# Threshold attention and a feed-forward block on one core: where summed weights are kept, when they and v are loaded, and the order of four products

## The chip, the cores and the metric

The kernel runs on one core of a Trainium2 chip. The time is the device time of one execution in microseconds (us), as the median of several runs: 1335.26 us over three runs (1334.43 to 1337.13). A profile is one more execution, recorded by the hardware profiler.

## What is computed

For each of 8 batches and 8 heads (576 tokens, 64 features a head) the attention keeps only the scores within `tau` of a row's maximum. The result is the input of a normalised two-layer block with 512 features in, 2048 hidden, 512 out. All data are float32.

```
scores = q @ k.T / 8
scores = where(scores >= max(scores) - tau, scores, -1e9)
attn = exp(scores - max); attn = attn / (sum(attn) + 1e-9)
x = attn @ v                         # heads side by side: (8, 576, 512)
xn = (x - mean) / sqrt(var + 1e-6) * g_ln
out = x + relu(xn @ w_ch1) @ w_ch2
```

## The kernel before, in words

**Slots and groups.** Attention is cut into nine slots for each batch, numbered 0 to 8 here (72 in all): slots 0 to 3 and 5 to 8 are a pair of heads with half of the queries, slot 4 is the rest of the queries of all heads. The feed-forward block is cut into 16 groups of 288 tokens, two for each batch. Its steps are a generator, and the main loop deals them out to the four quarters of each slot (`second_part`, L1322, by `dealt` and `STEPS`), so that TensorE (PE) always has something to multiply between the pieces of attention. An even group takes slots 7 and 8 of its batch and 0 and 1 of the next; an odd group takes slots 2 to 6. In what follows group two is the even group of the second batch.

**One slot of attention.** PE makes the scores (L434); VectorE (DVE) takes the negated row maxima (L450); GpSimd (POOL) makes the threshold (L454); ScalarE (ACT) writes four exponentials into the tile `e` (L463); DVE masks them against the scores in four instructions (L473, "masks"); POOL divides them (L490); DVE transposes 32x32 blocks in place (L559). One DMA then stores `e` to a scratch tensor in DRAM (`scr<-e`, L580, 1152 KB), and in the next slot a DMA brings it back in another layout (`em<-scr`, L594, 1024 KB, and `er<-scr`, L599). PE multiplies that by v (L638, L649). There is one tile `e` for all slots, so the exponentials of a slot wait until the store of the slot before has landed.

**The SP queue.** Nearly all DMAs are issued by SyncE (SP), in the order in which the program names them. A wait of one holds all behind it. In a slot the order is: `em<-scr` and two `er<-scr`; four stores of results (`out_dram<-ot`); in slots 8, 0, 1 and 2 four loads of q and four of k for the next pair of heads (L120), which wait until DVE has transposed the old ones (L368 to L378); loads of summed weights (L891); the store `scr<-e`; in slots 7, 8, 0 and 1 the load of v for the next batch: `v_in` (L135, 256 KB) and two `v_rest` (L144, 32 KB each).

**Sums in place of products.** From group two on, a part of the first layer is made by a scheme of Winograd's kind. A "unit" (`unit`, L940) takes four of the 16 hidden tiles and makes them with seven products of half size instead of eight: 28 half steps instead of 16 whole ones. A whole step multiplies a 128x128 weight by 288 columns, a half step by 144. Each appears in the program as two matmuls of 64 columns of weights and in the trace as four MATMUL records. A group has three units (hidden tiles 0 to 3, 4 to 7 and 12 to 15) and four plain tiles (8 to 11). The second layer is made in the same manner from group one on, in seven segments (`second_quarters`, L1136).

A unit needs twelve 128x128 sums of weights (768 KB). They are made once, by DVE and POOL, from the weights (`sums_of_w1`, L893), one twelfth at every ninth step of group one's second layer, and stored in DRAM. Two rooms in SBUF take them in turn: room 0 is `extra[:, :12]`, room 1 is the rest of `extra`, the end of an unused `e` tile and `ident`, so that a load into room 1 is three DMAs. A room is refilled from DRAM for every unit of every group (`load_sums`, in quarter 1 of the slot after the unit, which is ahead of the masks).

The seven products of a unit are named p1 to p7. p6, p7 and the last one are added up in one PSUM bank (`chain`), and between them ACT copies it out (L979, L983). p3 and p5 have banks of their own. The order is p6, p5, p7, p3 in the first unit of a group and p5, p6, p3, p7 in the others (L994).

**Rooms that bound the order.** PSUM has two banks for the feed-forward block (`ps_ff`); a bank is free again when ACT has copied it out. After every group the means are subtracted by DVE (`centre`, L742), and the next group's first products wait for that.

Of the kernel before, what the change touches and what calls it, by code (L numbers as in the profile page):

```python
# [18 lines left out]
def kernel(  # L19
# [106 lines left out]
            tiles.append(t)  # L126
        loaded[u] = tuple(tiles)

    def load_v(u):
        b, hp = units[u]  # L130
        vt = ins.tile([128, 2, J, D], F32, tag="v", name="v_in")
        vr = v_rest[hp]
        both = v[b, 2 * hp : 2 * hp + 2]
        if b:
            nc.sync.dma_start(  # L135
                out=vt.rearrange("p h c d -> p h (c d)"),
                in_=both[:, : J * 128].rearrange("h (p c) d -> p h (c d)", c=J),
            )
        for h in range(0 if b else 2):
            nc.sync.dma_start(  # L140
                out=vt[:, h], in_=both[h, : J * 128].rearrange("(c p) d -> p c d", p=128)
            )
        for j in range(2):
            nc.sync.dma_start(  # L144
                out=vr[64 * j : 64 * j + 64, j], in_=both[:, J * 128 :].rearrange("h p d -> p h d")
            )
        values_in[u] = (vt, vr)
# [319 lines left out]
    def weights(n, es, thr, divide):  # L467


        den = small.tile([128, 4], F32, tag="den", name="den")  # L470
        for i in range(4):
            e = blocks_of(es, i, n)
            nc.vector.scalar_tensor_tensor(  # L473
                out=e, in0=like(blocks[i], n), scalar=thr[:, i : i + 1], in1=e,
                op0=ALU.is_ge, op1=ALU.mult, accum_out=den[:, i : i + 1],
            )
            if divide and i % 2:
                nc.vector.reciprocal(den[:, i - 1 : i + 1], den[:, i - 1 : i + 1])  # L478
        if not divide:
            nc.vector.reciprocal(den, den)  # L480
        diags = []
        for i in range(4):
            if not divide:
                if i % 2 == 0:
                    two = ffn.tile([128, TOK], F32, tag="o", bufs=4, name="diag")
                diags.append(two[:, i % 2 * 128 : i % 2 * 128 + 128])
                nc.scalar.mul(diags[i], ident, den[:, i : i + 1])
                continue
            e = blocks_of(es, i, n)
            nc.gpsimd.tensor_scalar(  # L490
                out=e, in0=e, scalar1=den[:, i : i + 1], scalar2=1.0,
                op0=ALU.mult, op1=ALU.mult,
            )
        return diags
# [350 lines left out]
                    yield  # L845

    UNITS = (((0, 1), (2, 3)), ((4, 5), (6, 7)), ((12, 13), (14, 15)))
    PLAIN = [d for d in range(ND) if all(d not in t for u in UNITS for t in u)]
    sums_due = []
    last_added = set()  # L850

    def unit_slots(g):
        n, i = divmod(ready(g), QUARTERS)
        return [n + (i > 0) + k for k in range(len(UNITS))]

    PIECES = 12
    stored = [
# [20 lines left out]
        at, pieces = [r for r in rooms_of(room) if r[0] <= i][-1]  # L878
        return pieces[:, i - at]

    def room_for(g, k):

        return (len(UNITS) * g + k) % 2

    def store_sums(k):
        for at, pieces in rooms_of(room_for(2, k)):
            nc.sync.dma_start(out=stored[k][:, at : at + pieces.shape[1]], in_=pieces)

    def load_sums(g, k):
        for at, pieces in rooms_of(room_for(g, k)):  # L890
            nc.sync.dma_start(out=pieces, in_=stored[k][:, at : at + pieces.shape[1]])  # L891

    def sums_of_w1():  # L893


        for k, (f1, f2) in enumerate(UNITS):
            for c in range(2):
                for m in range(2):
                    cols = [slice(128 * t[m], 128 * t[m] + 128) for t in (f1, f2)]
                    a11, a12 = (w1_sb[2 * j + c][:, cols[0]] for j in range(2))  # L900
                    a21, a22 = (w1_sb[2 * j + c][:, cols[1]] for j in range(2))
                    if k < 2:
                        p2, p3, p4 = (piece_of(room_for(2, k), i, c, m) for i in range(3))
                    else:
                        two = [ffn.tile([128, TOK], F32, tag="o", bufs=4, name="sum") for _ in range(2)]
                        p2, p3, p4 = two[0][:, :128], two[0][:, 128:256], two[1][:, :128]
                    for eng, out, a, b, op in (
                        (nc.vector, p3, a11, a21, ALU.subtract),
                        (nc.vector, a21, a21, a22, ALU.add),
                        (nc.vector, p2, a21, a11, ALU.subtract),  # L910
                        (nc.gpsimd, p4, a12, p2, ALU.subtract),
                    ):
                        eng.tensor_tensor(out=out, in0=a, in1=b, op=op)
# [3 lines left out]
            if k < 2:  # L917
                store_sums(k)

    sums_of_x = {}  # L920

# [18 lines left out]
    def unit(g, xc, k):  # L940


        f1, f2 = UNITS[k]
        t1, t2, t3, t4 = sums_of_x[g]
        of = lambda f, j: hidden[:, f[0] : f[0] + 2, (early, late)[j]]
        h11, h12, h21, h22 = of(f1, 0), of(f1, 1), of(f2, 0), of(f2, 1)
        w_of = lambda f, j: lambda c, m: w1_sb[2 * j + c][:, 128 * f[m] : 128 * f[m] + 128]
        s_of = lambda which: lambda c, m: piece_of(room_for(g, k), which, c, m)
        x_of = lambda i, j: lambda c: xc[:, 2 * i + c, (early, late)[j]]
        t_of = lambda t: lambda c: t[:, c]  # L950
        other = [
# [39 lines left out]
            steps(other[1], s_of(2), x_of(1, 1), True, True),  # L991
            lambda: sums_due.append(lambda: add(h12, other[1], h12)),
        )
        order = (p5, p6, p3, p7) if k else (p6, p5, p7, p3)  # L994
        for i, (part_of, after) in enumerate(order):
            for end in part_of:
                if end:
# [30 lines left out]

    def unit_and_load(g, k):
        yield from second_half(g, k)  # L1030
        n = max(now // QUARTERS, unit_slots(g)[k])
        yield from unit(g, centred[g], k)
        h, i = divmod(len(UNITS) * g + k + 2, len(UNITS))
        if h < NG:
            at_quarter(max(n, now // QUARTERS) + 1, 1, load_sums, h, i)

    def first_units(g):


        xc = centred[g]  # L1040
        sq = hidden[:, ND - NK :]
        due = False
        for k in range(2):
            for d in PLAIN[2 * k : 2 * k + 2]:
# [17 lines left out]
            yield from unit_and_load(g, k)  # L1062
            if k == 0:
                due = now >= QUARTERS * NS
                if not due:
# [70 lines left out]
    def second_quarters(g, rb):  # L1136
# [87 lines left out]
        t2 = "t2", 3, by_fours, dve if g == 1 else pool, b11, b11, b12, ALU.add  # L1224
        if g == 1:
            later(t3, urgent=pool)
            banks_taken[0] = True
        yield from segment(w2[0, 0], b11, y11)
        if g == 1:
            need("t3")  # L1230
            later(t2, urgent=dve)
        yield 2, 0.5
        if g > 1:
            yield from unit_and_load(g, 2)
            sums_of_x.pop(g)
# [46 lines left out]

    def ffn_steps(g):
        rb = yield from (first_part if g < 2 else first_units)(g)
        sums = sums_of_w1() if g == 1 else iter(())
        for i, step in enumerate((second_quarters if g else second_plain)(g, rb)):
            if i % 9 == 8:
                next(sums, None)
            yield step

# [3 lines left out]


    ROOM = (0.6, 1.0, 1.25, 0.35)
    STEPS = [0.5 + NK * ND * 2] + [0.5 + NK * ND * 2 - NK * ND // 8] + [
        0.5 + NK * ND * 2 - NK * ND // 8 - 2 * len(UNITS)
    ] * (NG - 2)
    ends = [sum(STEPS[: i + 1]) for i in range(NG)]  # L1300
    queue = []
    issued = part = now = 0
# [19 lines left out]
    def second_part(n, i):  # L1322
# [13 lines left out]
        else:  # L1336
            if i == 0:
                share = remain / (ready(g + 1) // QUARTERS - n)
                if has_unit and n < unit_slots(g)[2]:
                    dealt[:] = [4, 4, UNIT_COST - 2, 2]  # L1340
# [12 lines left out]
        least = 2 if has_unit and i < 2 and n < unit_slots(g)[2] else 0.5  # L1353
# [82 lines left out]
    for n in range(NS):  # L1436
# [49 lines left out]
        if n < SLOTS:  # L1486
            run_all(stores)
        conversion.begin_to(behind_at)
        run(n, 2)
        second_part(n, 2)  # L1490
        if n < FIRST:
# [93 lines left out]
```

## Time and profile before

| what | from | value |
|---|---|---|
| median of three runs | the times | 1335.26 us (1334.43 to 1337.13) |
| the profiled execution | the times | 1337.87 us |
| its span, first to last instruction | the page | 1336.1 us |
| granted TensorE clock, mean | the page | 0.990 |
| PE busy / DVE / ACT / POOL | the page | 1280.0 / 961.8 / 528.6 / 674.2 us |
| DMA engines, mean rate | the page | 186 GB/s, 248.06 MB |
| loads of sums | the page's DMA issues | 20 of 768 KB; 20 of 576 KB, 20 of 128 KB and 20 of 64 KB |
| store `scr<-e` | the page's DMA issues | 60 of 1152 KB, median 5.2 us to landing |

A busy PE is the union of its matmul records, so its idle time is what the first table of the page leaves: 1336.1 - 1280.0 = 56 us. "Waits" lists, for an engine and a line, who ended its idle time. A timeline row gives start, duration, engine, line and operation, and in brackets the idle time before it. A row of SPq is the issue of a DMA, not its transfer. A landing is told by the DMA views.

### The profile page before, as it was taken

Reading aid. Unit: us, or ns where it says so; the run is one execution under the profiler, and the core shown is the slowest. Engines: PE = TensorE matmul, PEld = TensorE weight load, DVE = VectorE, ACT = ScalarE, POOL = GpSimd, SP = SyncE. Lnnn points to the kernel's source line nnn. Section 1 sums busy time; section 2 is a strip of 40 time slices with the busy share of each in tenths; the row PEclk is TensorE's granted clock in tenths of the full one; section 3 lists DMA queues with packets and bytes.
Section 4 is the critical chain, followed back from the end, with each engine's and each line's share of the span. In section 5 each row is a group of like instructions: output and inputs, shape, how many; then the busy total and the mean of one; then the engine's idle time right before and its main releaser. Section 6 shows DMA issues by size and latency. Waiting matters only on the chain.

```text
span 1336.1 us, 45057 instructions
## 1 busy us (share of the span) xinstructions
PE 1280.0 (96%) x19320; PEld 1090.4 (82%) x19320; DVE 961.8 (72%) x1762; ACT 528.6 (40%) x1191; POOL 674.2 (50%) x890
## 2 busy tenths in 40 slices
PE   8899889889999999999999999999999999999997
PEld 6765457778898898988989888987979888898987
DVE  7979888985777858785877857777576857777123
ACT  5866342243433424342343424334243423434131
POOL 3465565544545454554535455453445545455423
PEclk9999899999999999999999999999999999999999
DMA  8937865567765776657666667648676576565311
GB/s 151 292 116 186 205 165 175 199 175 208 219 207 184 220 208 207 222 166 211 182 213 206 196 165 228 212 169 215 197 216 208 175 201 182 187 224 185 85 43 20
DMA packets 349144, 248.06 MB, mean 186 GB/s; under 512 B 248912, under 2 KB 301136, under 8 KB 340880
## 3 DMA queue, kind: packets, MB, share of 16 engines
q1 hardware_dynamic: 342832, 244.29, 61.9%
q8 instruction: 152, 2.49, 0.8%
q10 hardware_dynamic: 5952, 0.74, 0.4%
q0 software_dynamic: 160, 0.15, 0.1%
q14 instruction: 48, 0.39, 0.1%
HBM read 155.45 MB, written 89.65 MB: 183 GB/s over the span
## 4 chain that ended last, share of the span: by engine, by line
PE 66%; DMA 4%; DVE 3%; ACT 2%; POOL 2%; issue 2%; POOLq 0%; ACTq 0%; DVEq 0%; SPq 0%
PE seg L103 27%; PE chain L103 10%; PE p L103 8%; PE sc L434 7%; PE sc L638 7%; PE sc L103 5%; DMA scr<-e 4%; DVE e L473 2%; ACT e L463 1%; PE sc L649 1%; DVE neg L450 1%; POOL e L490 1%; DMA v_in<-in_v_dram 1%; POOL q_in L350 0%; POOL sum L692 0%
## 5 line engine op out<-in xcount | busy, mean ns | idle before, releaser
L450 DVE TENSOR_REDUCE neg<-sc 128x2 f32<-128x1152 f32 x144 | 190.0, 1353 | 153.9 <-PE sc L434 150.9
L490 POOL TENSOR_SCALAR e<-e,den 128x576 f32<-128x576 f32 x264 | 206.1, 792 | 116.8 <-DVE den L478 116.7
L103 PE MATMUL p<-xc,w 128*64 128x288 f32 (+1 forms) x2080 | 233.4, 374 | 18.8 <-ACT y L1181 13.9
L103 PE MATMUL seg<-hidden,w 128*64 128x144 f32 x3840 | 246.6, 287 | 0.0
L103 PEld LDWEIGHTS seg<-hidden,w 128*64 128x64 f32 x3840 | 234.6, 137 | 10.4 <-issue 10.2
L473 DVE SCALAR_TENSOR_TENSOR e<-sc,thr,e 128x576 f32<-128x576 f32 x288 | 222.4, 810 | 26.3 <-ACT e L463 13.2
L103 PEld LDWEIGHTS p<-xc,w 128*64 128x64 f32 x2080 | 139.4, 138 | 100.2 <-ACT y L1181 15.5
L463 ACT ACTIVATE e<-sc,neg 128x576 f32<-128x576 f32 x288 | 196.4, 754 | 22.2 <-DMA scr<-e 17.9
L559 DVE STREAM_TRANSPOSE e<-e 128x1152 f32<-128x1152 f32 (+1 forms) x113 | 163.8, 1451 | 22.8 <-POOL e L490 22.4
L1166 POOL TENSOR_TENSOR hidden<-hidden 128x576 f32<-128x576 f32 x88 | 122.6, 1419 | 97.4 <-ACT hidden L1008 88.6
L454 POOL TENSOR_SCALAR thr<-neg,low_sb 128x2 f32<-128x2 f32 x144 | 39.7, 276 | 252.8 <-DVE neg L450 250.8
L434 PE MATMUL sc<-kT,qT 64*64 64x384 f32 (+3 forms) x2048 | 139.6, 403 | 2.9 <-DVE e L473 1.6
L638 PE MATMUL sc<-em,v_in 128*64 128x128 f32 (+1 forms) x2368 | 131.9, 265 | 5.1 <-DVE e L473 3.0
L638 PEld LDWEIGHTS sc<-em,v_in 128*64 128x64 f32 x2368 | 122.9, 138 | 9.1 <-DVE e L473 4.5
L103 PE MATMUL seg<-hidden,stage 128*64 128x144 f32 x1920 | 123.1, 286 | 0.4 <-ACT part L1181 0.4
L103 PEld LDWEIGHTS seg<-hidden,stage 128*64 128x64 f32 x1920 | 117.2, 137 | 3.2 <-issue 2.5
L434 PEld LDWEIGHTS sc<-kT,qT 64*64 64x64 f32 x2048 | 76.6, 133 | 43.4 <-issue 21.2
L103 PE MATMUL chain<-t,extra 128*64 128x144 f32 x1344 | 99.2, 291 | 0.0
L1181 ACT COPY part<-seg 128x288 f32<-128x288 f32 x74 | 30.0, 407 | 156.1 <-PE seg L103 133.4
L103 PEld LDWEIGHTS chain<-t,extra 128*64 128x64 f32 x1344 | 86.8, 140 | 0.0
L663 ACT COPY x<-sc 128x128 f32<-128x128 f32 x120 | 31.1, 267 | 127.8 <-PE sc L434 71.3
L1022 POOL TENSOR_TENSOR hidden<-hidden 128x288 f32<-128x288 f32 x48 | 38.8, 808 | 75.4 <-ACT hidden L1386 73.9
(165 smaller groups left out, 1774.0 us busy)
## 6 DMA issues: line engine op xcount, KB each, us to landing
scr<-e SPq DMA_DIRECT2D x60, 1152.0 KB, 5.2
em<-scr SPq DMA_DIRECT2D x63, 1024.0 KB, 5.8
extra<-sums SPq DMA_DIRECT2D x20, 768.0 KB, 6.4
extra<-sums SPq DMA_DIRECT2D x20, 576.0 KB, 5.1
out_dram<-ot SPq DMA_DIRECT2D x248, 36.0 KB, 3.9
q_in<-in_q_dram SPq DMA_DIRECT2D x120, 72.0 KB, 2.5
er<-scr SPq DMA_DIRECT2D x132, 64.0 KB, 5.2
k_in<-in_k_dram SPq DMA_DIRECT2D x116, 72.0 KB, 2.9
```

Source lines behind the costliest of these rows:

```text
L103: nc.tensor.matmul(out[r], lhsT=lhsT[:, r], rhs=rhs, **flags)
L434: mm = nc.tensor.matmul(sc[h][64 * i : 64 * i + 64, at : at + n], lhsT=ql[r] if s == HP else qT[r, half, j * 128 + 64 * i : j * 128 + 64 * ...
L450: nc.vector.tensor_reduce(out=neg[:, i], in_=pairs[h], axis=AXL.X, op=ALU.max, negate=True,)
L454: nc.gpsimd.tensor_scalar(out=thr[:, i], in0=neg[:, i], scalar1=-1.0, scalar2=low_sb, op0=ALU.mult, op1=ALU.add,)
L463: nc.scalar.activation(blocks_of(es, i, n), like(blocks[i], n), func=AF.Exp, bias=neg[:, i : i + 1])
L473: nc.vector.scalar_tensor_tensor(out=e, in0=like(blocks[i], n), scalar=thr[:, i : i + 1], in1=e, op0=ALU.is_ge, op1=ALU.mult, accum_out=de ...
L490: nc.gpsimd.tensor_scalar(out=e, in0=e, scalar1=den[:, i : i + 1], scalar2=1.0, op0=ALU.mult, op1=ALU.mult,)
L559: nc.vector.transpose(et[:, :, at], et[:, :, at])
L638: mm = nc.tensor.matmul(dst[64 * h : 64 * h + 64], lhsT=vt[:, h, c, :], rhs=pick(em[:, 2 * j : 2 * j + 2, c], h), start=c == 0 and first, ...
L663: nc.scalar.copy(x_of(2 * b + (s > HP))[:, s % (HP + 1), 128 * j : 128 * j + 128], pv[j])
L1022: nc.gpsimd.tensor_tensor(out=sq[:, 0], in0=sq[:, 0], in1=sq[:, c], op=ALU.add)
L1166: eng.tensor_tensor(out=out[at], in0=in0[at], in1=in1[at], op=op)
```

## The change

1. **v.** In slots 7, 8, 0 and 1 the load of v for the next batch is issued ahead of the store `scr<-e` instead of behind it, and its first DMA (`v_in`) waits for the second of the slot's four masks.
2. **Rooms.** Room 1 holds the sums of the second unit for good. Room 0 is refilled for the first and third unit in turn, each time with one DMA of 768 KB, in quarter 2 of the slot after the unit, behind the second mask. That makes 25 loads instead of 40 (of one or three DMAs). In slots 8 and 1 the load stands behind v and ahead of `scr<-e`.
3. **Group two** has two units, and hidden tiles 12 to 15 are plain: three plain tiles ahead of each unit and two behind. No sums are loaded for it. The sums of the first two units are made in group one, at every 13th step; those of the third in group two's second layer, at every 24th step, and stored from there. Group two's second layer starts as group one's does.
4. **Order.** After the last slot all units have the order p6, p5, p7, p3.

```diff
+    masked = []
+
+    def behind_masks(request):
+        if masked:
+            tc.add_manual_dep(
+                request.ins, masked[-1].ins.name,
+                mybir.DependencyInfo(mybir.DependencyClass.Sync, mybir.DependencyReason.ANTI),
...
     def weights(n, es, thr, divide):
...
+            if i == 1:
+                masked[:] = [mask]
...
+    def load_sums(k):
+        behind_masks(nc.sync.dma_start(out=extra[:, :PIECES], in_=stored[k]))
+        in_room[0] = k
+
+    def units_of(g):
+
+        return 2 if g == 2 else 3
...
-        s_of = lambda which: lambda c, m: piece_of(room_for(g, k), which, c, m)
+        s_of = lambda which: lambda c, m: piece_of(k % 2, which, c, m)
...
-        order = (p5, p6, p3, p7) if k else (p6, p5, p7, p3)
+        order = (p5, p6, p3, p7) if k and now < QUARTERS * NS else (p6, p5, p7, p3)
...
     def unit_and_load(g, k):
         yield from second_half(g, k)
-        n = max(now // QUARTERS, unit_slots(g)[k])
         yield from unit(g, centred[g], k)
-        h, i = divmod(len(UNITS) * g + k + 2, len(UNITS))
-        if h < NG:
-            at_quarter(max(n, now // QUARTERS) + 1, 1, load_sums, h, i)
+        if k == 1 or g == 2 or (g, k) == (NG - 1, 2):
+            return
+        if now < QUARTERS * NS:
+            at_quarter(now // QUARTERS + 1, 2, load_sums, 2 - k)
+        else:
+            load_sums(2 - k)
...
+        tiles = ((8, 9, 10), (11, 12, 13), (14, 15)) if g == 2 else ((8, 9), (10, 11), ())
...
-        sums = sums_of_w1() if g == 1 else iter(())
+        sums = sums_of_w1({1: (0, 1), 2: (2,)}.get(g, ()))
         for i, step in enumerate((second_quarters if g else second_plain)(g, rb)):
-            if i % 9 == 8:
+            if i % (13 if g == 1 else 24) == (12 if g == 1 else 23):
                 next(sums, None)
...
         conversion.begin_to(behind_at)
+        if n >= SLOTS - 2 and (n + 2) % SLOTS < HP and n < NS - 2:
+            load_v((n + 2) // SLOTS * HP + (n + 2) % SLOTS, behind_masks)
         run(n, 2)
         second_part(n, 2)
...
-        elif n >= SLOTS - 2 and (n + 2) % SLOTS < HP and n < NS - 2:
-            load_v((n + 2) // SLOTS * HP + (n + 2) % SLOTS)
```

More of the change, by code (lines that the diff above doesn't have):

```diff
@@ L127, in load_qk, with load_v @@
         loaded[u] = tuple(tiles)
-    def load_v(u):
+    masked = []
[4 more added lines that the diff above has]
+                mybir.DependencyInfo(mybir.DependencyClass.Sync, mybir.DependencyReason.ANTI),
+                reason="not beside the turned weights",
+            )
+    def load_v(u, behind=lambda request: None):
         b, hp = units[u]
@@ L134, in load_v @@
         if b:
-            nc.sync.dma_start(
-                out=vt.rearrange("p h c d -> p h (c d)"),
-                in_=both[:, : J * 128].rearrange("h (p c) d -> p h (c d)", c=J),
+            behind(
+                nc.sync.dma_start(
+                    out=vt.rearrange("p h c d -> p h (c d)"),
+                    in_=both[:, : J * 128].rearrange("h (p c) d -> p h (c d)", c=J),
+                )
             )
@@ L472, in weights @@
             e = blocks_of(es, i, n)
-            nc.vector.scalar_tensor_tensor(
+            mask = nc.vector.scalar_tensor_tensor(
                 out=e, in0=like(blocks[i], n), scalar=thr[:, i : i + 1], in1=e,
@@ L847 @@
     UNITS = (((0, 1), (2, 3)), ((4, 5), (6, 7)), ((12, 13), (14, 15)))
-    PLAIN = [d for d in range(ND) if all(d not in t for u in UNITS for t in u)]
     sums_due = []
@@ L853, in unit_slots @@
         n, i = divmod(ready(g), QUARTERS)
-        return [n + (i > 0) + k for k in range(len(UNITS))]
+        return [n + (i > 0) + k for k in range(units_of(g))]
     PIECES = 12
@@ L879, in piece_of, with sums_of_w1 @@
         return pieces[:, i - at]
[L881 to L896, printed above, removed]
+    in_room = [0]
+    def load_sums(k):
[3 more added lines that the diff above has]
+        return 2 if g == 2 else 3
+    def sums_of_w1(which):
+        for k in which:
+            f1, f2 = UNITS[k]
             for c in range(2):
@@ L902, in sums_of_w1 @@
                     if k < 2:
-                        p2, p3, p4 = (piece_of(room_for(2, k), i, c, m) for i in range(3))
+                        p2, p3, p4 = (piece_of(k, i, c, m) for i in range(3))
                     else:
@@ L916, in sums_of_w1 @@
                     yield
-            if k < 2:
-                store_sums(k)
+            if k == 0:
+                nc.sync.dma_start(out=stored[k], in_=extra[:, :PIECES])
     sums_of_x = {}
@@ L940, in unit @@
     def unit(g, xc, k):
+        assert k == 1 or in_room[0] == k
         f1, f2 = UNITS[k]
@@ L1041, in first_units @@
         sq = hidden[:, ND - NK :]
+        tiles = ((8, 9, 10), (11, 12, 13), (14, 15)) if g == 2 else ((8, 9), (10, 11), ())
         due = False
-        for k in range(2):
-            for d in PLAIN[2 * k : 2 * k + 2]:
+        for k in range(3):
+            for d in tiles[k]:
                 bank = ps_ff.tile([128, 512], F32, tag="ff", name="p1")
@@ L1061, in first_units @@
                 yield 2, 1
-            yield from unit_and_load(g, k)
+            if k < 2:
+                yield from unit_and_load(g, k)
             if k == 0:
@@ L1223, in second_quarters @@
         t3 = "t3", 3, by_fours, pool, b12, b22, b12, ALU.subtract
-        t2 = "t2", 3, by_fours, dve if g == 1 else pool, b11, b11, b12, ALU.add
-        if g == 1:
+        t2 = "t2", 3, by_fours, dve if g < 3 else pool, b11, b11, b12, ALU.add
+        if g < 3:
             later(t3, urgent=pool)
@@ L1228, in second_quarters @@
         yield from segment(w2[0, 0], b11, y11)
-        if g == 1:
+        if g < 3:
             need("t3")
@@ L1232, in second_quarters @@
         yield 2, 0.5
-        if g > 1:
+        if g > 2:
             yield from unit_and_load(g, 2)
-            sums_of_x.pop(g)
             later(t3, t2, urgent=pool)
@@ L1296 @@
     ROOM = (0.6, 1.0, 1.25, 0.35)
-    STEPS = [0.5 + NK * ND * 2] + [0.5 + NK * ND * 2 - NK * ND // 8] + [
-        0.5 + NK * ND * 2 - NK * ND // 8 - 2 * len(UNITS)
-    ] * (NG - 2)
+    STEPS = [0.5 + NK * ND * 2] + [
+        0.5 + NK * ND * 2 - NK * ND // 8 - (2 * units_of(g) if g > 1 else 0) for g in range(1, NG)
+    ]
     ends = [sum(STEPS[: i + 1]) for i in range(NG)]
@@ L1338, in second_part @@
                 share = remain / (ready(g + 1) // QUARTERS - n)
-                if has_unit and n < unit_slots(g)[2]:
-                    dealt[:] = [4, 4, UNIT_COST - 2, 2]
+                if has_unit and n < unit_slots(g)[0] + 2:
+                    dealt[:] = [4, 8 if g == 2 else 4, UNIT_COST - 2, 2]
                 elif has_unit:
@@ L1352, in second_part @@
         got = 1 if i in (0, QUARTERS - 1) else 3 if i == 2 and has_unit else 2
-        least = 2 if has_unit and i < 2 and n < unit_slots(g)[2] else 0.5
+        least = 2 if has_unit and i < 2 and n < unit_slots(g)[0] + 2 else 0.5
         while queue and (owed >= least or got == 3 or got == 1 and whole):
```

## The prediction, made before the changed kernel was run

> **What bounds the kernel now.** I read the page's busy table first, then who ended the waits of PE and ACT, then the timeline and the DMA landings around the longest of these.
>
> ```profile
> PE 1280.0 (96%) x19320; PEld 1090.4 (82%) x19320; DVE 961.8 (72%) x1762; ACT 528.6 (40%) x1191; POOL 674.2 (50%) x890
> ```
> ```profile
> PE p L103 <- ACT y L1181: 13.9, 6, 3.1
> ...
> PE p L103 <- DVE xc L742: 3.5, 4, 2.4
> PE sc L638 <- DVE e L473: 3.0, 4, 1.3
> PE chain L103 <- ACT hidden L1057: 2.6, 1, 2.6
> ...
> PE chain L103 <- ACT hidden L983: 1.5, 3, 0.5
> ```
>
> PE is the bound: 56 us of the span are idle. The largest group is six waits, 13.9 us, one in slot 0 of each batch from the third on. One of them in the timeline:
>
> ```profile
> 600.89 2.63 SPq L120 DMA_DIRECT2D k_in<-in_k_dram  x4
> 603.57 0.62 SPq L891 DMA_DIRECT2D extra<-sums  x1
> 605.03 0.36 SPq L580 DMA_DIRECT2D scr<-e  x1
> 605.43 0.44 SPq L135 DMA_DIRECT2D v_in<-in_v_dram  x1
> 605.91 2.78 SPq L144 DMA_DIRECT2D v_rest<-in_v_dram  x2
> ```
> ```profile
> 614.18 2.64 ACT L463 ACTIVATE e<-sc,neg 128x576 f32<-128x576 f32 x4 [3.08 <-DMA scr<-e]
> ...
> 616.70 0.42 ACT L1181 COPY y<-seg 128x288 f32<-128x288 f32 x1
> ...
> 617.16 2.19 PE L103 MATMUL p<-xc,w 128*64 128x144 f32 x16 [2.71 <-ACT y L1181]
> ```
> ```profile
> 613.20:617.10 3.90, 1.26 (x22) 0.99 (x17) 2.41 (x7) 2.92 (x6) 0.00 (x0) 0.97 0.49 101
> 617.16:620.26 3.10, 3.10 (x26) 3.06 (x28) 3.04 (x7) 0.25 (x1) 2.61 (x4) 0.50 1.11 313
> ```
>
> In slot 8 the load of sums goes out at 603.57, the store of `e` at 605.03. The store lands 9.1 us later, at 614.1; in a slot with nothing beside it (issue at 667.81) it takes 4.2. ACT needs `e` back at 611.1, waits 3.08 us, runs four exponentials, and only then frees the bank that PE waits for: 2.71 us. Then the seventh column of the windows, the granted clock, reads 0.50 for 3.4 us, which costs another 1.7. The six waits are 2.09, 0.38, 2.71, 3.13, 2.67 and 2.89; the last four are each followed by such a piece. The skill's page "TensorE: Matmul & The Clock Gate" (Part 1) puts the threshold at about 3.4 us without activity; here 2.67 were enough and 2.09 were not, so by the page a stall of this size would cost its own length alone, and the trace decides otherwise.
>
> DMAs of the SP queue land in the order of their issue here: sums 6.5 us after issue (610.0), store 614.1, v 9.4 after issue (614.8), the `v_rest` behind. So whatever stands ahead of the store in slot 8 is paid by PE.
>
> **The change part by part.** The built order shows DVE, ACT, POOL and PE unchanged from group three to the last slot, rooms apart. What moves there is the SP queue.
>
> *Slot 8 (five times: -0.5 to +3.2 us each, taken +1.2).* The hold is empty there: the second mask ends at 600.2, and SP is busy with `k_in` until 603.5. So v, its two rests and the sums go out from 603.57, all ahead of the store. The bytes ahead of it grow by 256 + 64 KB; at the store's pace behind the sums (1152 KB in 614.1 - 610.0 = 4.1 us) that is 1.1 us. By issue it is more: 0.44 for `v_in` and two `v_rest` at 0.6 (slot 7) to 1.4 (605.91, two in 2.78) put the sums back by 1.8 to 3.2. In three of the five, a packet of instructions of 0.93 to 0.96 us sits on one DMA engine between the store's packets and delays its end by about 1; PE's stream gets 96 records shorter, so the packet comes at another place and may miss the store: -0.5 then. I take 1.2, nearest to the bytes, since the queue still drains `k_in` at 605.6: 5 x 1.2 = +6.0. The skill's "DMA: Bandwidth & Descriptors" (Rules for kernel authors) says to issue a DMA early and wait late; by that rule v ahead of the store costs nothing, and the sum would be 6.0 lower. The rows above show why it fails here: the store, whose landing somebody awaits, shares the queue.
>
> *Slots 7, 0, 1, 3, 5: nothing.* Slot 7: SP is idle before the store at 744.0; the mask ends at 739.2 and v is through first. Slot 0: the store goes out 1.8 later; it landed at 630.9 and the exponentials started at 636.4. Slot 1: v's 320 KB come ahead, 768 KB of sums go; it landed 1.4 before it was needed (0.3 in the tightest batch). Slot 3: one load of 768 KB for three, held until 677.2 instead of 676.5; the store landed 0.6 ahead of need. Slot 5 loses 768 KB. Behind each held DMA only the store and the next slot's DMAs queue. The covers of slots 1 and 3 are thin: if gone, some 0.5 us a batch, 3 in all.
>
> *Group one to group two (-2 to -7.6, taken -5.5).* The trace has PE waiting 0.65 and 1.34 at 241 to 243 on DVE's masks, 0.22 at 259, then
>
> ```profile
> 261.55 0.29 DVE L913 TENSOR_TENSOR sum<-w 128x128 f32<-128x128 f32 x1 [1.81 <-DMA sums<-sum]
> ...
> 267.29 4.10 PE L103 MATMUL p<-xc,w 128*64 128x288 f32 x32 [2.41 <-DVE xc L742]
> ...
> 274.00 1.20 PE L103 MATMUL chain<-xc,w 128*64 128x144 f32 x16 [2.60 <-ACT hidden L1057]
> ```
>
> and 0.36 at 275: 7.58 us. DVE is late each time, and ahead of it stand sums of weights (three DVE steps, 0.9 us, up to 3 beside POOL), the last of which even wait 1.81 for their own stores. In the new order one set fewer stands ahead of the masks of slot 3 of that batch, two fewer ahead of those of slot 4, and the third unit's four sets are gone. That brings DVE forward by more than PE's 2.0 at 243 and about 3 more at `xc`, so the first four waits (4.62) go. The wait at 274.00 is ACT's order, not DVE's alone: the copy of the first plain tile ends about 6.2 us after `xc` starts PE, and PE has 4.1 of work. 2.1 less what `xc` is early leave about 1.9, now in front of the third plain tile, which covers the 0.36. 7.58 - 1.9 = 5.7, and I take 5.5, since `em<-scr` now has the store of room 0 (768 KB) ahead of it and landed only just in time before (258.80, used at 258.93). If DVE's gain is eaten by contention with POOL, 2 remain.
>
> *The half-speed piece at 275.6 to 278.9: -1.7.* It follows the two long waits; 1.9 alone is under 2.09, which had none. Zero if they stay.
>
> *Slot 0 of group two (308.25): -2.1.* No sums are loaded in slot 8 there, so the store has 768 KB less and 320 KB more ahead of it. Zero if another wait follows.
>
> *Group two's third unit as plain tiles: +1.0.* 16 whole steps for 28 half steps. Eight whole steps take 4.10 us (x32 above): 0.513 each, so 2 more are 1.03. The twelve DVE sums, 0.3 us each, move to its slots 0 and 1, where DVE waits 2.2 for the mean at 343.78 and masks are needed 7 us later: covered; uncovered, 2.
>
> *End: -1.5.* Three units wait 0.50 for ACT's copy after p7; with p3 in between (16 records, 0.98 us to the next) the copy of 0.40 is covered. Their loads are in place: the last went out at 1282.3 and is used at 1299.5.
>
> *Fewer loads (25 for 40):* nothing but slots 1 and 5 above.
>
> Sum: +6.0 - 5.5 - 1.7 - 2.1 + 1.0 - 1.5 = -3.8. Against the profiled execution, 1337.87, that is 1334.1; the median of the runs lies 2.6 lower, at 1335.26, so the forecast is **1331.5**.
>
> **Rivals.**
> 1. *v ahead of the store deepens the wait (slower).* Place: slot 8 of five batches. Price: 3.2 us each if the rests go out at 1.4, 16 us, against gains of 10.8 - 1.0: +6.2, 1341.5. It decides from about 2.0 us a batch. For: 1.4 is what the rests took in that very slot. Against: there they were issued behind 1920 KB.
> 2. *The early gains turn into the next wait (no change).* Of the entry to group two only 2 remain, the half-speed piece stays: +6.0 - 2 - 2.1 + 1.0 - 1.5 = +1.4, 1336.7. For: ACT's order alone left 2.1 there. Against: four late sets of sums really go.
> 3. *The waits of slot 0 go after all,* the hold doing what it says: the five last waits, 11.8, and four half-speed pieces, 6.8, go as well: -18.6 - 9.8 = -28.4, 1306.9. Against: SP's own rows, 600.89 to 603.5.
>
> **How the numbers follow.** Forecast 0.47, rival 1 0.25, rival 2 0.20, rival 3 0.08. What a measurement can tell from no change is 0.2%, 2.7 us. Faster: 0.41 of the forecast, 0.04 of rival 2, 0.07 of rival 3: 0.52. Slower: 0.21 of rival 1, 0.04 of rival 2: 0.25. The rest 0.23. The forecast's own range is 1326 to 1336. The whole range leaves out rival 3 and the far end of rival 1 (with nothing gained at the entry): 1323 to 1342.
>
> **What would show it.** `extra<-sums` in slot 8 issued behind two `v_rest`, and the store landing 10 us or more after the last `k_in`; ACT waits for `scr<-e` in five slots 0 of 4 us, PE's of 3 to 4.5, each with a clock of 0.50 behind it; no wait on `xc` at group two and no half-speed piece there; no waits on L983's copy at the end. I am wrong if the store of slot 8 lands earlier after its scores than now, if new waits stand in group two's slots 0 and 1, or if slots 1 or 3 begin to wait for `scr<-e`.

## The result, and the profile after

The changed kernel takes 1343.65 us (median; 1342.22 to 1344.57), the kernel before, measured beside it, 1334.85 us. The ratio is 1.0062, with a 95% interval of 1.0044 to 1.0079: slower, by 0.6%. The forecast was 1331.5, with a range to 1342.0. The profiled execution took 1344.57 us with a span of 1342.8; before it was 1337.87 and 1336.1, so the two profiles differ by 6.7 us, and those are to be placed.

The busy table on the page of the changed kernel:

```profile
PE 1281.8 (95%) x19272; PEld 1091.6 (81%) x19272; DVE 960.9 (72%) x1760; ACT 526.0 (39%) x1189; POOL 671.9 (50%) x888
```

PE has 48 records less and is busy 1.8 us longer, and it is idle for 61 us in place of 56. From the waits (engine, line, who ended the idle time: us in total, times, longest) those that matter:

```profile
PE p L103 <- ACT y L1198: 21.9, 5, 5.0
...
PE seg L103 <- DVE hidden L1183: 7.0, 1, 7.0
...
DVE sum L925 <- DMA out_dram<-ot: 4.3, 1, 4.3
```

The first is the group of slot 0 that took 13.9 us in six waits (L1181 is L1198 now). One of the six has gone, that of group two; the other five have nearly doubled, from 11.8 to 21.9. The second did not exist. At the entry to group two the wait of 2.41 on `xc` has gone, and in place of the 2.60 on a hidden tile at 274 one of 1.56 stands at 263.66. The three waits on the copy of L983 at the end have gone too.

The same place as the prediction's, slot 8 into slot 0 of the fifth batch, in the timeline of the changed kernel: first what SP issues, then ACT, then PE.

```profile
603.64 3.24 SPq L120 DMA_DIRECT2D k_in<-in_k_dram  x4
606.98 0.57 SPq L146 DMA_DIRECT2D v_in<-in_v_dram  x1
607.60 1.30 SPq L156 DMA_DIRECT2D v_rest<-in_v_dram  x2
608.94 0.59 SPq L897 DMA_DIRECT2D extra<-sums  x1
609.63 0.38 SPq L594 DMA_DIRECT2D scr<-e  x1
619.36 0.37 SPq L608 DMA_DIRECT2D em<-scr  x1
```
```profile
619.39 2.63 ACT L475 ACTIVATE e<-sc,neg 128x576 f32<-128x576 f32 x4 [5.42 <-DMA scr<-e]
621.89 0.41 ACT L1198 COPY y<-seg 128x288 f32<-128x288 f32 x1
```
```profile
622.36 2.19 PE L103 MATMUL p<-xc,w 128*64 128x144 f32 x16 [5.04 <-ACT y L1198]
```

v and its two rests take SP 1.96 us, from 606.98 to 608.94, and only then do the sums go out. The store lands at 619.3, ACT has waited 5.42 for it (3.08 before), and PE waits 5.04 (2.71 before).

The new wait is in slot 1 of the batch in which group two ends. One row of SP (four stores of results), then the DVE rows:

```profile
319.35 1.96 SPq L815 DMA_DIRECT2D out_dram<-ot  x4
```
```profile
317.64 0.28 DVE L925 TENSOR_TENSOR sum<-w 128x128 f32<-128x128 f32 x1
...
325.17 0.29 DVE L925 TENSOR_TENSOR sum<-w 128x128 f32<-128x128 f32 x1 [4.33 <-DMA out_dram<-ot]
...
326.03 0.81 DVE L485 SCALAR_TENSOR_TENSOR e<-sc,thr,e 128x576 f32<-128x576 f32 x1
...
329.37 1.41 DVE L1183 TENSOR_TENSOR hidden<-hidden 128x576 f32<-128x576 f32 x2
```

A sum for the third unit waits 4.33 us for stores of results; the last of the four lands at 325.04. The masks (L485) and the sums of hidden tiles (L1183) stand behind it in DVE's order, and PE waits 6.95 us for the latter.

Both traces, cut where DVE starts the row maxima of each slot (L450 and L462; the 72 slots are counted through from 0 here), give the account of the 6.7 us:

| stretch | before | after | difference |
|---|---|---|---|
| start to slot 13 | 216.4 | 215.3 | -1.2 (1.0 of it where a half-speed piece near 153 is 3.4 us long in place of 6.8) |
| slots 13 to 18, entry to group two | 86.8 | 80.2 | -6.6 |
| slot 18 to 19 (slot 0 of group two) | 23.4 | 19.6 | -3.8 |
| slot 19 to 20 (its slot 1) | 21.9 | 29.8 | +7.9 |
| the five later stretches that hold slot 0's wait | 125.0 | 138.2 | +13.2 |
| slot 71 to the end | 116.7 | 114.5 | -2.1 |
| all others | | | -0.7 |

The second to fourth rows belong together, since PE's steps are dealt to these slots anew. Its records there are 48 fewer: 32 more in slots 13 to 17, 56 fewer in slot 18, 24 fewer in slot 19. So of the -3.8 in slot 18 the wait is 2.1, and the other 1.7 is work that now stands elsewhere or is gone.

### The profile page after: what moved, and what is told of

Read it like the earlier page. It is cut to its first block, busy times and chain, and to the rows that moved or that the text cites. A ratio compares the mean times of both kernels' runs of the same rounds, so it can differ in the third digit from the quotient of the medians.

```text
span 1342.8 us, 44902 instructions
## 1 busy us (share of the span) xinstructions
PE 1281.8 (95%) x19272; PEld 1091.6 (81%) x19272; DVE 960.9 (72%) x1760; ACT 526.0 (39%) x1189; POOL 671.9 (50%) x888
## 4 chain that ended last, share of the span: by engine, by line
PE 67%; DMA 4%; DVE 3%; POOL 2%; issue 2%; ACT 2%; SPq 0%; POOLq 0%; DVEq 0%; ACTq 0%
PE seg L103 27%; PE chain L103 10%; PE p L103 10%; PE sc L446 7%; PE sc L652 7%; PE sc L103 5%; DMA scr<-e 4%; DVE e L485 2%; PE sc L663 1%; ACT e L475 1%; POOL e L504 1%; DVE neg L462 1%; DVE hidden L987 1%; POOL q_in L362 0%; DMA out_dram<-ot 0%
## 5 line engine op out<-in xcount | busy, mean ns | idle before, releaser
L462 DVE TENSOR_REDUCE neg<-sc 128x2 f32<-128x1152 f32 x144 | 190.1, 1353 | 150.1 <-PE sc L446 147.4
L103 PE MATMUL p<-xc,w 128*64 128x288 f32 (+1 forms) x2128 | 241.5, 377 | 25.2 <-ACT y L1198 21.9
L485 DVE SCALAR_TENSOR_TENSOR e<-sc,thr,e 128x576 f32<-128x576 f32 x288 | 222.5, 810 | 34.3 <-ACT e L475 21.2
L103 PEld LDWEIGHTS p<-xc,w 128*64 128x64 f32 x2128 | 144.0, 139 | 109.4 <-ACT y L1198 23.3
L1183 POOL TENSOR_TENSOR hidden<-hidden 128x576 f32<-128x576 f32 x86 | 120.5, 1426 | 95.0 <-ACT hidden L1021 86.2
L1198 ACT COPY part<-seg 128x288 f32<-128x288 f32 x74 | 30.0, 405 | 164.1 <-PE seg L103 144.9
L1035 POOL TENSOR_TENSOR hidden<-hidden 128x288 f32<-128x288 f32 x48 | 38.9, 811 | 81.7 <-ACT hidden L1402 80.2
```

Of the source, the lines that this page charges most:

```text
L103: nc.tensor.matmul(out[r], lhsT=lhsT[:, r], rhs=rhs, **flags)
L462: nc.vector.tensor_reduce(out=neg[:, i], in_=pairs[h], axis=AXL.X, op=ALU.max, negate=True,)
L485: mask = nc.vector.scalar_tensor_tensor(out=e, in0=like(blocks[i], n), scalar=thr[:, i : i + 1], in1=e, op0=ALU.is_ge, op1=ALU.mult, accum ...
L1035: nc.gpsimd.tensor_tensor(out=sq[:, 0], in0=sq[:, 0], in1=sq[:, c], op=ALU.add)
L1183: eng.tensor_tensor(out=out[at], in0=in0[at], in1=in1[at], op=op)
```

## The experiments

Theory A: what SP issues ahead of the store `scr<-e` in slot 8 is paid by PE in the next slot 0. Theory C: the wait in slot 1 of group two comes from the tiles that the third unit's sums share with the stores of results. The rivals are B (v costs nothing there; something else deepened the waits) and D (twelve sums more are too much for DVE). In the expectations the letters stand for the theories of that run alone.

**Three orders of the SP queue.** e1 puts v back:

```diff
         conversion.begin_to(behind_at)
-        if n >= SLOTS - 2 and (n + 2) % SLOTS < HP and n < NS - 2:
-            load_v((n + 2) // SLOTS * HP + (n + 2) % SLOTS, behind_masks)
...
             load_v(s + 1)
+        elif n >= SLOTS - 2 and (n + 2) % SLOTS < HP and n < NS - 2:
+            load_v((n + 2) // SLOTS * HP + (n + 2) % SLOTS)
```

> The changed kernel with one part undone: the load of v goes back behind the store `scr<-e`, without a hold; the sums of slot 8 stay ahead of the store. Theory A (the SP queue: what is issued ahead of the store of slot 8 is paid by PE in the next slot). In the changed kernel the sums of slot 8 go out 2.0 us later than they would without v (603.57 behind the last k_in by 0.67 before, 2.7 now), so the store should land about 2 us earlier after the masks than now, the five waits of PE for ACT's y (4.93, 5.04, 4.96, 4.33, 2.65) should shrink to about 2 to 3.3 each, and one or two of the double half-speed pieces should become single: 10 to 15 us less than 1343.65, 1329 to 1334. Theory B (rival: v costs nothing there; the waits deepened because the two-unit group moved the whole program against the packets of instructions): waits stay at 4.3 to 5.0, 1341 to 1345. Both: the wait of 6.95 at 323 in group two stays.

e2 leaves v ahead and moves the sums behind the store; e3 does both:

```diff
-            at_quarter(now // QUARTERS + 1, 2, load_sums, 2 - k)
+            at_quarter(now // QUARTERS + 1, 3, load_sums, 2 - k)
```

> The changed kernel with the loads of sums moved one quarter on, behind the store `scr<-e` of their slot; v stays ahead of the store. Theory A: 768 KB less ahead of the store in slot 8; the sums landed 5.3 us behind v's last rest (610.41 to 615.06 is 4.65, 770.46 to 775.30 is 4.84), so the store lands some 4.5 us earlier and the waits of PE fall to 0 to 0.6 in the five slots 0; their half-speed pieces go too (13.7 us of half speed behind four of them and more, 12 in sum). About 20 + 10 = 30 us less: 1313 to 1318. Theory B (rival: the store is slow by itself in that slot, or the em<-scr that then has the sums ahead of it becomes what PE waits for): less than 8 us gained, 1336 or more, with new waits of PE for em<-scr.

> The changed kernel with both the load of v and the loads of sums behind the store `scr<-e`. Theory A: no DMA of the change is left ahead of the store in slot 8, the wait of ACT for scr<-e goes in all five slots 0, with it all 21.9 us of waits and about 10 us of half speed: 1311 to 1316, a little under the run with the sums alone behind. Theory B (the next transfer takes the place of the one moved): em<-scr of slot 0 comes 3 to 4 us later behind the sums, PE waits for em instead, and the time is not under 1325.

Measured: e1 1329.23 us (ratio to the kernel before 0.9946, 0.9928 to 0.9964), e2 1318.43 (0.9865, 0.9849 to 0.9880), e3 1315.46 (0.9842, 0.9826 to 0.9859). The five waits of PE for ACT's y are 3.53, 3.90, 2.67, none and 1.36 in e1; 1.62, 1.69, 0.29 and none twice in e2; 1.19 and then none in e3. The two waits of e2 are longer than the 0.6 expected, and its time is 0.4 over the range; e1 and e3 lie within theirs. In e2 and e3 no half-speed piece is left between 338 and the last slots' end. SP in the same slot of e3:

```profile
602.65 0.63 SPq L120 DMA_DIRECT2D k_in<-in_k_dram  x1
603.88 0.36 SPq L594 DMA_DIRECT2D scr<-e  x1
604.28 0.43 SPq L897 DMA_DIRECT2D extra<-sums  x1
604.76 0.91 SPq L146 DMA_DIRECT2D v_in<-in_v_dram  x1
605.71 2.14 SPq L156 DMA_DIRECT2D v_rest<-in_v_dram  x2
609.28 0.38 SPq L608 DMA_DIRECT2D em<-scr  x1
```

The row of `em<-scr` tells when the store has landed, since it waits for that: 5.4 us after the store's issue here, 9.7 in the changed kernel. Theory A holds, and PE has no wait for `em<-scr` after the first 200 us in e1, in e2 and, but for 0.29 us at 211, in e3. B falls.

**Is it the issue or the bytes?** e9 moves only the two `v_rest` behind the store, by splitting them off `load_v` (the edit inside `load_v` is left out here):

```diff
...
+        rests = []
...
-            load_v((n + 2) // SLOTS * HP + (n + 2) % SLOTS, behind_masks)
+            load_v((n + 2) // SLOTS * HP + (n + 2) % SLOTS, behind_masks, rests)
...
             load_v(s + 1)
+        for part_of in rests:
+            part_of()
```

> The changed kernel with only the two `v_rest` (32 KB each) back behind the store; `v_in` (256 KB) stays ahead. It asks what v costs in slot 8: the time that SP takes to issue, or the bytes. Issue account: the store's issue, 8.47 us after the first mask as a mean of five slots (6.42 before), comes 1.25 us earlier (two rows of 0.62 to 0.63), and so does its landing; it lands 3.7 after ACT needs it in place of 5.0: 6 us less and one or two half-speed pieces, 1333 to 1339. Bytes account: 64 KB of 1088 ahead of the store are worth 0.2 us each, it lands 4.7 to 5.0 late, 1341 to 1346.

e12 does the mirror of e1: the kernel before with its load of v ahead of the store (and so behind the sums, which stand in quarter 1 there):

```diff
         conversion.begin_to(behind_at)
+        if n >= SLOTS - 2 and (n + 2) % SLOTS < HP and n < NS - 2:
+            load_v((n + 2) // SLOTS * HP + (n + 2) % SLOTS)
...
-        elif n >= SLOTS - 2 and (n + 2) % SLOTS < HP and n < NS - 2:
-            load_v((n + 2) // SLOTS * HP + (n + 2) % SLOTS)
```

> The kernel before with only the load of v ahead of the store `scr<-e`, without a hold. Theory A by the issue account: the store of slot 8 goes out and lands 2.0 us later in six batches (the first, group two's, has v and the sums too), PE's waits of 2.09, 0.38, 2.71, 3.13, 2.67 and 2.89 become 2.4 to 5.2, some half-speed pieces double: +12 to +18, 1348 to 1355. Theory B (v costs nothing there, and the deeper waits came with the room that is refilled): within 3 us of 1336.

e9: 1336.15 us (1.0006, 0.9985 to 1.0027 of before), and the store lands 3.9 us after it is needed: the issue account's 3.7, not the bytes' 4.7 to 5.0. e12: 1340.59 us (1.0026, 1.0006 to 1.0046), 4.5 us more than before. That is a miss of theory A as it was put (+12 to +18), and not B's answer either. Its SP rows in the same slot:

```profile
605.37 0.62 SPq L891 DMA_DIRECT2D extra<-sums  x1
606.03 0.43 SPq L135 DMA_DIRECT2D v_in<-in_v_dram  x1
606.51 1.31 SPq L144 DMA_DIRECT2D v_rest<-in_v_dram  x2
607.91 0.54 SPq L580 DMA_DIRECT2D scr<-e  x1
```

The landings tell more. Means over slot 8 of five batches, in us from the start of its first mask. The first row maxima of the next slot, which the exponentials wait for as well, end at 12.16 in all of them, and the last column counts from there (ACT itself is free at 12.36 to 12.46):

| kernel | SP's order | sums issued | store issued | store landed | late by |
|---|---|---|---|---|---|
| before | sums, store, v | 5.39 | 6.42 | 15.11 | 2.95 |
| changed | v, rests, sums, store | 7.61 | 8.47 | 17.14 | 4.98 |
| e1 | sums, store, v | 5.60 | 6.65 | 15.05 | 2.89 |
| e9 | v, sums, store, rests | 6.02 | 6.68 | 16.06 | 3.90 |
| e12 | sums, v, rests, store | 5.45 | 8.05 | 15.63 | 3.47 |
| e2 | v, rests, store, sums | 8.26 | 7.61 | 13.47 | 1.31 |
| e3 | store, sums, v | 6.88 | 6.44 | 12.10 | -0.06 |

Where the sums stand ahead of the store, it lands 9.4 to 10.2 us after the issue of the *sums*, whatever the store's own issue: in e12 that comes 1.6 us later than before, and the landing 0.5. So v ahead of the sums costs its issue: the sums go out 2.2 us later and the store lands 2.0 later, while the sums take 6.0 us from issue to landing in both kernels. With v between them the store follows the sums by 4.9 us in place of 3.7, about the 1.1 of the prediction's bytes; but the sums landed 0.7 sooner after their issue in e12, for a reason that no run shows, and 0.5 is left. A mean of five stores is not good to that much: in e1 and in the kernel before, with one order, single stores land between 12.8 and 16.7. In e3 one store is 1.8 late and four are 0.4 to 0.8 early. And the 768 KB of sums themselves cost 3.7 (changed kernel against e2) or 3.0 (e1 against e3).

**The kernel before.** e7 moves all its loads of sums behind the store; e10 moves only that of slot 8, by a condition in the same line (not shown):

```diff
-            at_quarter(max(n, now // QUARTERS) + 1, 1, load_sums, h, i)
+            at_quarter(max(n, now // QUARTERS) + 1, 3, load_sums, h, i)
```

> The kernel before with one edit: its loads of sums move from quarter 1 to quarter 3, behind the store `scr<-e` of their slot; nothing else of the change. Theory A (the sums ahead of the store make the waits of slot 0 in the kernel before too): the six waits of 2.09, 0.38, 2.71, 3.13, 2.67 and 2.89 fall to 0 to 0.5 and the four half-speed pieces behind them go: 11 + 6.8 = 18 us less, 1316 to 1321. Theory B (they come from the store itself, or from the 40 loads of two rooms, which would then delay em<-scr): 1330 or more.

> The kernel before with only the load of sums of slot 8 behind the store `scr<-e`; every other load of sums stays in quarter 1. Theory A (in the kernel before the waits of slot 0 come from that one load): as in the run with all loads of sums behind (1317.13), 1316 to 1321, no wait for ACT's y over 0.5 and no half-speed piece behind one. Theory B (the loads of the other slots took part): 1324 or more.

e7 took 1317.13 us (0.9848, 0.9833 to 0.9864), e10 1317.92 (0.9852, 0.9823 to 0.9881). In e7 the last unit of the last group is multiplied with another unit's sums, because its load comes behind it; the work is the same. In both, no wait of PE for ACT's y of 0.15 us or more is left in slot 0, and no half-speed piece between 280 and the end of the last slot. So one load, in one slot of a batch, had made all of the largest group of waits in the kernel before.

**The wait in group two.** e4 makes the third unit's sums in room 0, which is idle there, and so in no tile that a store uses:

```diff
-                    if k < 2:
-                        p2, p3, p4 = (piece_of(k, i, c, m) for i in range(3))
-                    else:
-                        two = [ffn.tile([128, TOK], F32, tag="o", bufs=4, name="sum") for _ in range(2)]
-                        p2, p3, p4 = two[0][:, :128], two[0][:, 128:256], two[1][:, :128]
+                    p2, p3, p4 = (piece_of(k % 2, i, c, m) for i in range(3))
...
-                    for i, piece in enumerate((p2, p3, p4) if k == 2 else ()):
-                        nc.sync.dma_start(out=stored[k][:, (i * 2 + c) * 2 + m], in_=piece)
+                    if k == 2 and c == m == 1:
+                        nc.sync.dma_start(out=stored[k], in_=extra[:, :PIECES])
+                        at_quarter(now // QUARTERS + 1, 3, load_sums, 0)
```

> The changed kernel, but group two makes the sums of its third unit in room 0 (idle there behind the first unit) instead of in the four tiles that the stores of results use as well; one store of 768 KB for twelve small ones, and one load to bring the first unit's sums back. Theory C (the DVE sum at 325.17 waits 4.33 us because its tile is still being stored by out_dram, and the masks and the sums of hidden tiles wait behind it in DVE's order): the 6.95 us wait of PE at 323.30 goes and the half-speed piece of 6.8 us behind it (3.4 us) with it: some 10 us less, 1332 to 1335. Theory D (rival: twelve sums more are simply too much work for DVE in slots 0 and 1): the wait stays at 5 us or more, 1341 to 1345. The five waits of PE in the later slots 0 stay in both.

e5 leaves the tiles and moves the sets of sums in time:

```diff
-            if i % (13 if g == 1 else 24) == (12 if g == 1 else 23):
+            if i % 13 == 12 if g == 1 else i in (20, 32, 43, 95):
```

> The changed kernel with the four sets of sums of group two's third unit at other steps of its second layer (20, 32, 43 and 95 of 112 in place of 23, 47, 71 and 95): the two sets that stood ahead of the masks of slot 1 of the batch (DVE rows at 317.64 and 325.17) move back into slot 0, behind its masks; the tiles stay the ones that the stores of results use. Theory C (those two sets, one by its work and one by its wait of 4.33 for out_dram, hold the masks and the sums of hidden tiles up): the wait of 6.95 goes wholly, so does the half-speed piece behind it, and the slot that took 29.8 us takes 21.9: some 8 to 10 us less, 1333 to 1336. Theory D (twelve more sums are too much for DVE wherever they stand): a wait of 2 us or more stays in these two slots, 1337 or more.

In e4 the first unit of group three is multiplied with the third unit's sums, because the load that brings its own back comes behind it; the work is the same. The wait falls from 6.95 to 2.43 us, the half-speed piece goes, and the stretch of slot 1 falls from 29.8 to 23.0. The median, 1340.75 (1.0035, 1.0016 to 1.0054 of before), fell by less than expected, since the five waits of slot 0 are longer in it (24.3 in place of 21.9; the five stretches that hold them take 142.3 in place of 138.2), for a reason that no run shows. So C is right for about two thirds of the wait. What is left fits the two sets' own work ahead of the masks, 0.9 us each, which is D's part. In e5 both go: 0.27 us of wait is left, the stretch takes 21.2, at the price of 0.6 in the slot ahead of it (which e6, with the same sets, does not show). Its median is 1337.00 (1.0009, 0.9993 to 1.0025 of before), 6.7 under the changed kernel, just over what C expected and at the 1337 that D named; but D's wait of 2 us or more is not there, and that decides.

**The hold.** e8 empties it:

```diff
-        if masked:
+        if False:
```

> The changed kernel without the hold: v and the sums are issued in the same places of SP's order, but wait for no mask. Theory A (in slot 8 SP is still busy with k_in when the second mask ends, so the hold is empty there; in the others the store comes behind the third transpose anyway): the same as the changed kernel, 1341 to 1346, with the five waits of 2.6 to 5.4. Theory B (the hold itself makes v late and with it the sums and the store): 5 us or more less, 1338 or under.

1345.46 us (1.0055, 1.0036 to 1.0073 of before), waits of 4.24, 4.80, 5.16, 2.65 and 3.96: nothing that can be told from the changed kernel. The order does it, not the wait for the mask.

**The end.** e11 changes only the order there:

```diff
-        order = (p5, p6, p3, p7) if k else (p6, p5, p7, p3)
+        order = (p5, p6, p3, p7) if k and now < QUARTERS * NS else (p6, p5, p7, p3)
```

> The kernel before with only the order of the last units' products changed (p6, p5, p7, p3 after the last slot). Forecast's step: the three waits of 0.50 for ACT's copy at the end go, 1.5 us of the stretch from slot 71 to the end, which took 116.7 in the trace of before and 114.5 in that of the changed kernel. Rival: another wait stands in their place and the stretch stays within 0.5 of 116.7. The median can't tell 1.5 us; the trace's stretch can.

The stretch from slot 71 to the end took 114.5 us in place of 116.7, and its idle time fell from 1.96 to 0.45: the three waits.

**All together.** e6 joins e3 and e5.

> The changed kernel with v and the loads of sums behind the store `scr<-e` and the sets of sums of the third unit at the other steps: the runs e3 and e5 together. If the two causes are apart, as theories A and C have it, their gains add: 1315.46 less 8 to 10, 1305 to 1308. Rival: once the late slots wait no more something else binds in group two (em<-scr behind the new stores, or DVE), and less than 4 us of it arrive: 1312 or more.

1306.50 us (1305.24 to 1307.29), ratio 0.9770 (0.9755 to 0.9786) to the kernel before: faster than both kernels, and 9.0 under e3, so the two causes add. Its busy line:

```profile
PE 1269.5 (97%) x19272; PEld 1079.6 (83%) x19272; DVE 961.6 (74%) x1760; ACT 527.1 (40%) x1189; POOL 672.4 (52%) x888
```

PE has the changed kernel's 19272 records and is busy 12 us less. In the changed kernel it was busy for 24.4 us at half speed between 200 and 1230 us, which is 12.2 us of work at full speed; in e6 there is no half-speed piece in that stretch. The idle time is 34 us.

## Why the prediction was wrong, step by step

- **Slot 8, +6.0: the step that failed.** It cost +13.2. The prediction had two sums for it, 1.1 by bytes and 1.8 to 3.2 by issue, and took 1.2, "nearest to the bytes". The landing moved by 2.0: by issue, since v stands ahead of the sums and these set when the store lands. e9, whose landing and time came out as the issue account had them, tells the two apart. Of the 13.2, 10.1 are the waits themselves. The other 3.1 fit the clock (PE is busy at half speed for 19.8 us there in place of 13.3): three of the five waits draw a half-speed piece of 6.8 us where there was one of 3.4 or none, and one lost its piece. Rival 1 had the mechanism and the place. Its price, 16 us, came near, but not by its own working: the rests went out at 0.65 us each and not at 1.4, the landing moved by 2.0 and not by 3.2, and the clock, which it did not price, made up part of the rest. That its total, 1341.5, is near the measured 1343.65 is luck, since it has nothing for the next step.
- **The twelve DVE sums in group two, "covered; uncovered, 2": the other failure.** +7.9: 6.95 of wait and 2.3 of half speed behind it (PE is busy for 4.6 us in it), less what the 24 records that left the slot took. Only their work was costed. That their tiles are those of the stores of results, which in slot 1 go out just ahead of them, was not looked at; the 1.81 us wait shown at 261.55 was a hint of the kind. The list of what would prove the forecast wrong had it (new waits in group two's slots 0 and 1), but no case gave it a price. That is why the range, which took rival 1 with all gains, ended 1.65 us too low.
- **Group one to group two, -5.5 - 1.7 + 1.0 = -6.2:** -6.6 measured, but the near match is in part luck. PE's idle time fell by 7.0 (8.5 to 1.56; 1.9 was forecast to stay), and the half-speed piece is gone. Rival 2 falls.
- **The +1.0 in it was mis-sized.** It took a half step as half of a whole one, 0.26 us. The row at 274.00 shows 16 records, four half steps, in 1.20: 0.30 each. So 28 of them are 8.4 us and 16 whole ones 8.2. Leaving out what half speed added, PE is busy about 1 us less in slots 13 to 19, not 1 more.
- **Slot 0 of group two, -2.1:** -3.8. The wait is gone as forecast; the rest is work dealt to other slots or gone, as above.
- **End, -1.5:** -2.1, and e11 gives the same with that edit alone.
- **Slots 7, 0, 1, 3, 5, nothing; the hold empty in slot 8:** right. The other stretches differ by 0.7 in all, and in e8, with no hold, the time and the waits stay. Rival 3, the hold doing what it says, falls.

Between the two profiles the three gains make -12.5 (forecast -9.8), and the two steps that failed +21.1 (forecast +6.0).

Left open: single stores land up to 2.3 us earlier or later than the mean of their kernel. The prediction put a part of that to packets of instructions on one DMA engine, and the traces bear it out as far as a comparison can. In the eight traces with the sums just ahead of the store, the 40 stores of slot 8 land either 2.5 to 2.8 us behind the sums (19) or 3.4 to 4.3 (21). In all of the 21 a 16 KB packet of instructions started 2.1 to 4.6 us before the landing, in the 19 only three times. No run here took the packets away.

## What to carry to other kernels

On a queue whose DMAs land in order, as all of SP's did in these 14 traces, put first the one that somebody waits for, and look at what the DMA just ahead of it is and when *that* goes out: v cost 2.0 us where it delayed the large load in front of the store, and 0.5 where it came behind that load. When work is moved to another place, price its buffers as well as its instructions: who holds the tile that it will write there? And a wait that repeats in every batch may hang on one DMA; moving that one alone (e10) took 18 us off the kernel before, while the whole change added 9.

## What the runs showed of the hardware

The half-speed pieces lie on a grid: in all 14 profiles they start whole multiples of 3.413 us apart and, but for the one that the end of each record cuts short, last 3.4, 6.8 or 10.2 us. Between 200 and 1230 us, 49 windows of that grid at full speed were followed by one at half speed; PE was idle for 1.88 us or more in each. None of the other 4108 had more than 2.02 idle, so the bound lies near 1.9 to 2.0 us. From a half-speed window the bound is lower: after 20 with 0.79 us or more idle the next was half again, after 49 with 0.72 or less it was full. So a wait is judged by how the grid cuts it. Windows of the changed kernel: busy time of PE, PEld, DVE, ACT, POOL, then the granted clock, DMA share and GB/s.

```profile
618.15:621.56 3.41, 0.00 (x0) 0.00 (x0) 0.77 (x3) 2.17 (x4) 0.00 (x0) 1.00 0.18 52
621.57:624.97 3.40, 2.61 (x22) 2.57 (x24) 3.33 (x11) 1.04 (x3) 2.12 (x3) 0.50 1.06 335
624.98:628.38 3.40, 3.40 (x32) 3.34 (x30) 2.27 (x3) 0.00 (x0) 2.17 (x3) 0.50 0.55 88
628.40:631.80 3.40, 3.40 (x62) 3.40 (x62) 1.37 (x3) 0.80 (x2) 0.00 (x0) 1.00 0.66 106
```
```profile
1092.60:1096.00 3.40, 1.87 (x32) 1.60 (x27) 1.50 (x5) 1.86 (x3) 0.57 (x1) 1.00 0.25 54
1096.02:1099.42 3.40, 2.30 (x38) 2.31 (x40) 3.33 (x11) 1.35 (x4) 1.81 (x3) 1.00 1.01 325
```

A wait of 5.04 us empties one window and leaves 0.8 idle in the next: two windows at half speed follow. The wait of 2.65 at 1094.47 is cut into 1.5 and 1.1, and none follows, while of the 2.67 at 927.03 in the kernel before 2.24 fell into one window, and a piece followed. The Trainium skill ("TensorE: Matmul & The Clock Gate", Part 1) has the free-running window of about 3.4 us, which agrees; its rule that the clock drops after an idle window differs from what was measured: 1.9 to 2.0 us idle of 3.4 was enough here, and the measurement decides.
